# Lightning attention and a leaky-ReLU feed-forward in one Trainium2 kernel: some places of a hand-written order are exchanged

## The chip, the cores and the metric

The kernel runs on one NeuronCore of one Trainium2 chip. The metric is device time in microseconds: the median over runs of the same kernel, smaller is better. The core has a matrix engine (TensorE, PE in the profile, with its weight loads as PEld), a vector engine (VectorE, DVE), a scalar engine (ScalarE, ACT), a general one (GpSimd, POOL) and SyncE (SP), which in this kernel issues nearly all of the DMA transfers, one after the other, from one queue. Each engine runs its own instructions in their order and waits on semaphores for the others.

## What is computed

The reference is block-wise attention with a decaying state, then a two-layer feed-forward. Shapes: 4 batches, 8 heads, 768 positions, 64 per head; the feed-forward takes 3072 tokens of 512, a hidden width of 2048, and gives 3072 x 512, all in 32-bit floats.

```python
for b in range(nb):                      # blocks of 64 positions, per batch and head
    intra = (q_b @ k_b.T) * Dmask        # lam ** (i - j) below the diagonal
    out_b = intra @ v_b + (q_b * lam_pow) @ kv_state
    kv_state = lam ** 64 * kv_state + (k_b * rev_pow).T @ v_b
x = out.transpose(0, 2, 1, 3).reshape(3072, 512)
h = x @ w_in                             # 512 x 2048
y = np.maximum(0.01 * h, h) @ w_out      # 2048 x 512
```

The two weight matrices arrive as 64-bit floats.

## The kernel before, in words

**Tiling.** The tokens are handled as 24 chunks of 128 (two attention blocks each; six chunks make a batch, numbered c = 0 to 23), four chunks make a group g of 512 tokens, and the hidden width is cut into eight blocks p of 256. The feed-forward's operands are split in three parts (h, l, m for x as xh, xl, xm, and for the weights as wh, wl, wm), so that each product of 32-bit precision is made of three products on PE.

**Stages.** Per chunk: load k, q and v; transpose k and q on PE (`transposes`, L550) or, for q of chunks 8 and 9 and for most of the later q and k, load them in 32 KB blocks (`load_subs`, L513) in such an arrangement that DVE can finish the transpose (`turn`, L522); the scores and the state's increment (`scores`, L410), their masking and the state's update (L643, L648, L650 on DVE, L653 on POOL); the outputs (`outputs`, L410), where a tiny copy L682 lies between two halves of the matmuls; and the split of the outputs into xh (L698, ACT), xl (L706, DVE) and xm (L724, DVE). k is scaled in place (L591) and q into another buffer (L598). Per weight block p: two 512 KB loads of 64-bit words (`to_float32`, L787), their conversion with three steps on ACT (L799, L801, L803) and two on DVE (L805, L806), and the split into wh, wm, wl (`parts`, L813 or L815, L818, L820). Per group and block: twelve matmuls per half (`up`, L856), an eviction with the leaky ReLU on ACT (L883), and a store of the result to a DRAM buffer G (L886). After about 340 us the second layer (`down`, L922) reads G back, splits it (L903, L904, L906) and multiplies.

**What sets the order.** No step is issued where it stands in the code. `Plan.add` numbers the operations in the order in which the code creates them, and `emit` issues them in the order of the list `ORDER` (L266): its 1296 entries are pairs of an operation's number and its engine, and a negative number stands for filler matmuls. What the list leaves out follows by a planner that uses the costs written in the calls of `add`. Only the order within one engine reaches the chip as an order; across engines, dependencies become semaphore waits. But `resolve` hands out the interchangeable buffers (four PSUM banks `pt`, `b10`, `b11`, `b2`; `low0` and `low1`; the raw buffers) in the list's order over all engines, so a changed list can exchange their names:

```python
for at, n in enumerate(program):
    ...
    able = [x for x in self.kinds[s.kind] if holds[x] is None or not holds[x].left]
    s.name = ... min(able, key=lambda x: ended[x])
```

The operations that the change and the steps of the prediction name, with the instruction of the profile and the start of each in the profiled execution of the kernel before:

| operation | engine, line | what it is | start, us |
|---|---|---|---|
| 43, 53 | PE L410, L550 | outputs of chunk 1, first half; transpose of q of chunk 2 | 16.87, 16.28 |
| 97, 104, 96, 98 | ACT L801, L803, L799, L803 | conversions of the first two weight halves | 13.39, 14.01, 14.63, 15.19 |
| 188 | PE L550 | transpose of k of chunk 7 | 47.63 |
| 250 | PE L856 | up, group 0, block 2, product xm, wm, first half | 51.38 |
| 272, 270 | SP L513 | q blocks of chunks 8 and 9 | 44.29, 46.80 |
| 349, 325, 355 | SP L787 | loads of weight halves (block 7, block 4, block 4) | 47.35, 48.77, 57.85 |
| 277 | SP L513 | q block | 47.77 |
| 281, 271, 280, 278 | SP L513 | q blocks | 49.22 to 52.32 |
| 283, 208 | SP L466, L528 | k of chunk 8 (two issues), v of chunk 7 | 52.43, 53.42 |
| 267, 274, 276, 279, 282 | SP L513 | q blocks | 54.53 to 57.76 |
| 268, 273, 269, 275 | SP L513 | q blocks | 58.29 to 60.24 |
| 247 | SP L886 | store of the hidden tokens of group 0, block 0 | 60.28 |
| 304, 303 | SP L466, L528 | k of chunk 9, v of chunk 8 | 60.84, 62.33 |
| 326, 327, 328 | ACT L799, L801, L803 | conversion of load 325 | 54.54, 55.13, 55.78 |
| 255, 351, 288 | ACT L883, L801, L682 | eviction of block 2, second half; conversion of load 349; copy in the outputs of chunk 6 | 56.40, 57.29, 60.20 |
| 202, 197 | DVE L598, L706 | scaling of q of chunk 7; xl of chunk 5 | 58.51, 53.55 |
| 206, 330, 336 | DVE L650, L806, L806 | state of chunk 6; second DVE step of loads 325 and 331 | 55.60, 56.56, 57.19 |
| 337, 338, 339 | DVE L815, L818, L820 | wh, wm, wl of block 4 | 57.90, 59.11, 60.67 |
| 289 | PE L410 | state's increment of chunk 7, which reads v of load 208 | 60.04 |
| 340, 344, 341, 345, 346 | PE L856 | up, group 0, block 4: two products with wh, two with wl, one with wm | 61.18 to 66.02 |
| 305 | PE L550 | transpose of k of chunk 9 (load 304) | 66.89 |

The weight blocks named here are those of `w_in`. Loads 325 and 331 are the two halves of block 4, 349 and 355 those of block 7.

Of the kernel before, what the change touches and what calls it, by code (L numbers as in the profile page):

```python
# [239 lines left out]
def kernel(  # L240
# [117 lines left out]
    plan = Plan(kinds, also, {"k@2": early[0], "v@2": early[0], "k@3": early[1], "v@3": early[1], "q@3": early[2]})  # L358
    plan.fill, plan.idle, plan.warm, plan.order = busy, None if ORDER else busy, 1.3 + 0.22 * WARM, ORDER
    add = plan.add  # L360
# [688 lines left out]
```

## Time and profile before

| | |
|---|---|
| median of 3 runs | 606.58 us (606.28 to 606.84) |
| the profiled execution's own time | 607.09 us |
| its span, first to last instruction | 605.3 us |
| mean granted TensorE clock | 0.999 |
| PE busy | 596.8 us (99% of the span) |
| DVE, ACT, POOL busy | 298.7, 208.9, 73.0 us |
| DMA | 105.18 MB, of it 104.30 MB on SP's queue |

A row of the timeline gives the start and the length in us, the engine (a q behind it: its queue, issuing), the line, the operation, the tiles as out<-in, the shapes and a count; in brackets stands how long the engine was idle before it, and what ended that. Tile names have their buffer numbers left out, so `b` is any of three PSUM banks. Rows of one engine that follow each other closely with the same line and tiles are merged. The row of a DMA on SP covers only its issue; the time to landing stands in the rows on DMA issues.

### The profile page before, as it was taken

The numbers are of one execution on the slowest core, as the hardware profiler recorded it, in microseconds if no ns is written. First come the engines' busy times: TensorE is split into PE (matmuls) and PEld (weight loads), VectorE is DVE, ScalarE is ACT, GpSimd is POOL, SyncE is SP. The second block draws the span as 40 slices with busy tenths as digits, with TensorE's granted clock in tenths as the row PEclk, the third lists the DMA queues.
The fourth block names the chain that finished last, engine by engine and source line by source line (L and its number), as shares of the span: only waits on it lengthen the run. The fifth ranks groups of instructions, "written<-read, shape, count | busy, mean of one in ns | idle before, by whom it ended". The sixth has DMA issues, their size and how long they took to land.

```text
span 605.3 us, 12711 instructions
## 1 busy us (share of the span) xinstructions
PE 596.8 (99%) x5362; PEld 491.9 (81%) x5362; DVE 298.7 (49%) x410; ACT 208.9 (35%) x322; POOL 73.0 (12%) x85
## 2 busy tenths in 40 slices
PE   8899999999999999999999999999999999999997
PEld 5787788888888888887888888888888888888886
DVE  6999755360454434344166855354353543534430
ACT  3676661212433433435334421222312313214111
POOL 3332132241322032140000000000000000000000
PEclk9999999999999999999999999999999999999999
DMA  9998887597888798664875833424433333434201
GB/s 219 225 271 190 232 248 198 89 256 180 222 223 203 225 251 236 176 208 175 322 267 181 307 105 125 154 90 138 120 113 131 115 129 122 124 103 125 84 1 69
DMA packets 149993, 105.18 MB, mean 174 GB/s; under 512 B 125872, under 2 KB 126640, under 8 KB 149936
## 3 DMA queue, kind: packets, MB, share of 16 engines
q1 hardware_dynamic: 149648, 104.30, 59.8%
q8 instruction: 42, 0.69, 0.5%
q14 instruction: 15, 0.12, 0.1%
q10 hardware_dynamic: 288, 0.07, 0.0%
HBM read 68.69 MB, written 35.65 MB: 172 GB/s over the span
## 4 chain that ended last, share of the span: by engine, by line
PE 93%; DMA 3%; SPq 2%; DVE 1%; issue 1%; POOL 0%; DVEq 0%; POOLq 0%
PE b L856 31%; PE b L922 16%; PE psc L922 11%; PE po L922 11%; PE pt L856 10%; PE pt L922 5%; PE po L410 4%; PE psc L410 3%; DMA att<-in_k_dram 3%; SPq L513 1%; PE b L349 1%; PE po L550 1%; PE b L550 0%; POOL att L591 0%; PE pt L349 0%
## 5 line engine op out<-in xcount | busy, mean ns | idle before, releaser
L904 DVE SCALAR_TENSOR_TENSOR xl<-att,xh 128x1024 fp32r<-128x1024 f32 x48 | 58.6, 1222 | 125.8 <-ACT xh L903 125.8
L903 ACT ACTIVATE xh<-att 128x1024 fp32r<-128x1024 f32 x48 | 50.9, 1061 | 147.5 <-PE po L922 73.9
L856 PE MATMUL b<-xl,wl 128*128 128x512 f32 (+1 forms) x296 | 78.1, 389 | 0.0
L856 PE MATMUL b<-xm,wm 128*128 128x512 f32 (+1 forms) x296 | 77.8, 390 | 0.0
L856 PE MATMUL b<-xh,wh 128*128 128x512 f32 (+1 forms) x296 | 77.3, 389 | 0.0
L883 ACT ACTIVATE gs<-b 128x512 f32<-128x512 f32 x73 | 42.9, 596 | 95.7 <-PE b L856 85.4
L856 PEld LDWEIGHTS b<-xl,wl 128*128 128x128 f32 x296 | 54.7, 188 | 11.6 <-DVE wl L820 0.4
L856 PEld LDWEIGHTS b<-xh,wh 128*128 128x128 f32 x296 | 54.5, 188 | 11.5 <-DVE att L598 0.3
L856 PEld LDWEIGHTS b<-xm,wm 128*128 128x128 f32 x296 | 54.4, 188 | 11.3
L906 DVE SCALAR_TENSOR_TENSOR xm<-xl,xh 128x1024 fp32r<-128x1024 f32 x48 | 58.8, 1225 | 4.7
L922 PE MATMUL b<-wh,xh 128*128 128x512 f32 x144 | 56.0, 389 | 0.0
L922 PE MATMUL b<-wl,xl 128*128 128x512 f32 x144 | 56.0, 389 | 0.0
L922 PE MATMUL b<-wm,xm 128*128 128x512 f32 x144 | 56.0, 389 | 0.0
L653 POOL TENSOR_TENSOR att<-att 128x256 f32<-128x256 f32 x40 | 29.1, 728 | 112.5 <-DVE att L650 76.6
L922 PE MATMUL psc<-wm,xm 128*128 128x512 f32 (+1 forms) x100 | 38.2, 387 | 0.0
L922 PE MATMUL po<-wm,xm 128*128 128x512 f32 (+1 forms) x100 | 37.9, 384 | 0.0
L922 PE MATMUL psc<-wh,xh 128*128 128x512 f32 x96 | 37.3, 389 | 0.0
L922 PE MATMUL psc<-wl,xl 128*128 128x512 f32 x96 | 37.3, 389 | 0.0
L922 PE MATMUL po<-wh,xh 128*128 128x512 f32 x96 | 37.3, 389 | 0.0
L922 PE MATMUL po<-wl,xl 128*128 128x512 f32 x96 | 37.3, 389 | 0.0
L410 PEld LDWEIGHTS po<-att 64*64 64x64 f32 x1408 | 26.9, 134 | 10.4 <-issue 8.0
L410 PE MATMUL po<-att 64*64 64x64 f32 x1408 | 32.9, 222 | 1.6 <-issue 0.9
(103 smaller groups left out, 858.9 us busy)
## 6 DMA issues: line engine op xcount, KB each, us to landing
att<-g SPq DMA_DIRECT2D x48, 512.0 KB, 3.4
g<-gs SPq DMA_DIRECT2D x47, 512.0 KB, 3.6
raw<-in_moe_w_in_dram SPq DMA_DIRECT2D x16, 512.0 KB, 5.4
raw<-in_moe_w_out_dram SPq DMA_DIRECT2D x16, 512.0 KB, 4.5
out_dram<-gs SPq DMA_DIRECT2D x23, 256.0 KB, 2.1
att<-in_k_dram SPq DMA_DIRECT2D x44, 128.0 KB, 4.0
att<-in_v_dram SPq DMA_DIRECT2D x22, 256.0 KB, 4.3
wo<-w SPq DMA_DIRECT2D x8, 512.0 KB, 3.9
```

Source lines behind the costliest of these rows:

```text
L349: nc.tensor.matmul(wide[:, :k, :], lhsT=ident, rhs=_bc(ident[:, 0:C2], 1, k), start=True, stop=True, skip_group_check=True)
L410: nc.tensor.matmul(dst[HALF[cols]], lhsT=lhsT[HALF[rows]], rhs=rhs[HALF[rows]], start=start, stop=True, skip_group_check=True)
L513: move(0.55, lambda o=o, z=z: nc.sync.dma_start(out=o.rearrange("j (m i) -> j m i", i=C4), in_=z.rearrange("(m j) i -> j m i", j=C4)), key ...
L550: nc.tensor.transpose(out=at[y], in_=src[:, 2 * y:2 * y + 2, :].rearrange("p a d -> p (a d)"), identity=ident)
L653: add("POOL", 0.62, lambda new=new, j=j: nc.gpsimd.tensor_tensor(state[(j + 1) % 4], new, _bc(lam_c, 2, D), op=ALU.mult), [f"st{j % 4}", " ...
L856: nc.tensor.matmul(dst, lhsT=w[z][:, kk * 2 * P + f * P:kk * 2 * P + (f + 1) * P], rhs=x[z][:, kk, toks], start=start and kk == 0, stop=kk ...
L883: add("ACT", ns, lambda b=b, r=r: nc.scalar.activation(out=r(), in_=b(), func=AF.Prelu, bias=0.0, scale=1.0, alpha=0.01), [kb], [kg], rank ...
L903: add("ACT", 1.05, lambda: nc.scalar.activation(out=h, in_=graw[j], func=AF.Copy, bias=0.0, scale=NEAR), reads, wr("h"))
L904: add("DVE", 1.215, lambda: nc.vector.scalar_tensor_tensor(l, graw[j], 1.0, h.bitcast(F32), op0=ALU.mult, op1=ALU.subtract), reads + [f"rh ...
L906: add("DVE", 1.215, lambda: nc.vector.scalar_tensor_tensor(m, l.bitcast(F32), -S, h.bitcast(F32), op0=ALU.mult, op1=ALU.add), [f"rh{j}", f ...
L922: nc.tensor.matmul(to[:, cols], lhsT=ring[j][z][:, f * T + tb * P:f * T + (tb + 1) * P], rhs=W[pp][z][:, f * d_model:(f + 1) * d_model][:, ...
```

## The change

Nothing but the list `ORDER` differs: 34 stretches of it, from entry 49 on to entry 318. No operation is added or removed, and no other line changes. What that does to each engine's own order:

- PE: 43 comes ahead of 53; 250 comes ahead of 188 and the outputs and scores behind it.
- ACT: 97 comes behind 104 and 96; 288 comes ahead of 351.
- DVE: 202 comes ahead of 197; 336 comes ahead of 206 and 330.
- SP, from load 154 (v of chunk 6) to load 303: before 272, 270, 349, 277, 325, 281, 271, 280, 278, 283, 208, 267, 274, 276, 279, 282, 355, 268, 273, 269, 275, 247, 304; after 275, 349, 277, 272, 270, 271, 278, 276, 280, 283, 325, 281, 267, 208, 268, 274, 279, 282, 355, 273, 247, 269, 304.
- POOL: the same.
- Buffers: for block 4, 340 now writes bank `pt` and 344 bank `b10` (exchanged), and `low0` and `low1` are exchanged from 351 on; the later users of both follow.

The other moved entries (51, 119, 71) pass only entries of other engines. The list around the changes, its lines broken here and equal stretches left out:

```diff
...
 (37, "DVE"), (102, "ACT"),
+(51, "DMA"),
 (39, "POOL"), (25, "DVE"), (105, "DVE"), (-6, "PE"), (42, "PE"),
-(53, "PE"),
 (43, "PE"), (103, "ACT"),
-(51, "DMA"), (97, "ACT"),
 (104, "ACT"), (96, "ACT"), (171, "DMA"),
+(97, "ACT"),
 (40, "DVE"), (106, "DVE"),
+(53, "PE"),
 (52, "PE"), (98, "ACT"),
...
 (114, "PE"), (79, "POOL"),
+(119, "DMA"),
 (63, "DVE"), (64, "POOL"),
...
 (81, "PE"), (88, "PE"),
-(119, "DMA"),
 (84, "DVE"), (175, "DVE"),
...
 (116, "ACT"), (215, "DMA"),
-(71, "DVE"),
 (217, "ACT"), (123, "PE"),
+(71, "DVE"),
 (166, "PE"), (94, "DVE"),
...
 (231, "ACT"), (154, "DMA"),
+(275, "DMA"),
 (248, "PE"), (226, "ACT"),
...
 (249, "PE"), (153, "DVE"),
+(250, "PE"),
 (152, "DVE"), (234, "DVE"),
...
 (190, "PE"), (191, "PE"),
-(272, "DMA"), (270, "DMA"),
 (349, "DMA"), (277, "DMA"),
...
 (195, "PE"), (235, "DVE"),
+(272, "DMA"), (270, "DMA"), (271, "DMA"), (278, "DMA"), (276, "DMA"), (280, "DMA"), (283, "DMA"),
 (325, "DMA"), (236, "DVE"),
...
 (201, "DVE"), (333, "ACT"),
-(250, "PE"),
 (199, "ACT"),
-(271, "DMA"),
 (261, "PE"), (204, "DVE"), (251, "ACT"),
-(280, "DMA"),
 (237, "DVE"), (205, "POOL"),
-(278, "DMA"),
 (334, "ACT"),
-(283, "DMA"),
 (238, "DVE"),
+(267, "DMA"),
 (208, "DMA"), (332, "ACT"),
+(202, "DVE"),
 (254, "PE"),
+(268, "DMA"),
 (197, "DVE"), (326, "ACT"),
-(267, "DMA"),
 (203, "DVE"), (335, "DVE"), (257, "PE"), (274, "DMA"),
+(279, "DMA"),
 (329, "DVE"), (327, "ACT"), (262, "PE"), (258, "PE"),
+(336, "DVE"),
 (263, "PE"),
-(276, "DMA"),
 (284, "PE"), (259, "PE"),
...
 (206, "DVE"), (330, "DVE"),
-(336, "DVE"),
 (287, "PE"), (289, "PE"), (290, "PE"), (255, "ACT"),
-(351, "ACT"), (279, "DMA"),
 (337, "DVE"), (282, "DMA"), (288, "ACT"),
-(202, "DVE"),
+(338, "DVE"), (351, "ACT"), (339, "DVE"),
 (355, "DMA"),
-(338, "DVE"), (268, "DMA"), (339, "DVE"),
 (273, "DMA"),
+(247, "DMA"),
 (269, "DMA"),
+(304, "DMA"),
 (207, "POOL"), (291, "PE"), (298, "DVE"), (340, "PE"), (344, "PE"),
-(275, "DMA"),
 (299, "DVE"), (292, "ACT"), (296, "POOL"),
-(247, "DMA"),
 (356, "ACT"), (341, "PE"), (439, "DVE"),
-(304, "DMA"),
 (350, "ACT"), (295, "ACT"),
...
```

2 lines of the change are left out of this document (1 added, 1 removed).

## Prediction

> **What bounds the kernel now.** I read the page's busy shares first, then the busy time by stretch, then TensorE's (PE) timeline for its idle gaps, and only then the SyncE queue (SP) and the vector engines around those gaps. A step named by a number is the operation of that number in the plan, as the table before this prediction lists them.
>
> ```profile
> span 605.3 us, 12711 instructions
> PE 596.8 (99%) x5362; PEld 491.9 (81%) x5362; DVE 298.7 (49%) x410; ACT 208.9 (35%) x322; POOL 73.0 (12%) x85
> ...
> 60.00:70.00 10.00, 9.13 (x232) 7.49 (x226) 6.33 (x11) 5.43 (x11) 2.31 (x3) 1.00 0.90 250
> 130.00:340.00 210.00, 210.00 (x2220) 173.55 (x2219) 93.88 (x155) 80.89 (x139) 36.51 (x41) 1.00 0.77 225
> ```
>
> In the last two rows (stretch, length, then busy time of PE, PEld, DVE, ACT, POOL, the clock, the DMA share) PE is busy all of 130 to 340 us: nothing there can absorb a shift, and the order of PE's work in it is unchanged. So a microsecond won or lost by PE before 70 us should reach the end whole. The change reorders work only between about 14 and 67 us, so PE's gaps in that stretch are all that can be won:
>
> ```profile
> 46.25 1.07 PE L856 MATMUL b<-xl,wl 128*128 128x512 f32 x4
> 47.63 0.75 PE L550 MATMUL po<-att 128*128 128x128 f32 x4 [0.32 <-DMA att<-in_k_dram]
> ...
> 51.38 1.09 PE L856 MATMUL b<-xm,wm 128*128 128x512 f32 x4
> 52.31 1.08 PE L856 MATMUL b<-xh,wh 128*128 128x512 f32 x4
> ...
> 59.98 0.98 PE L410 MATMUL psc<-att 64*64 64x64 f32 x54
> ...
> 61.18 1.19 PE L856 MATMUL b<-xh,wh 128*128 128x512 f32 x4
> ...
> 63.13 1.08 PE L856 MATMUL b<-xl,wl 128*128 128x512 f32 x4
> ...
> 64.95 1.07 PE L856 MATMUL pt<-xm,wm 128*128 128x512 f32 x4
> 66.89 0.76 PE L550 MATMUL po<-att 128*128 128x128 f32 x4 [0.87 <-DMA att<-in_k_dram]
> ```
>
> Both gaps (in brackets) stand before a transpose of k (188 at 47.63, 305 at 66.89) whose load comes late. 1.19 us together is nearly all there is.
>
> **Part 1: PE 43 ahead of 53, and the conversion step 97 two places later on ScalarE (ACT).** 97, 104 and 96 only change places among themselves on ACT; the last of the group, 98, still comes after the same work, so that costs 0. On PE the transpose 53 now comes behind the 16 small matmuls of 43:
>
> ```profile
> 16.87 0.46 PE L410 MATMUL po<-att 64*64 64x64 f32 x16
> 16.98 0.69 DVE L531 COPY att<-b 128x512 f32<-128x512 f32 x1 [0.65 <-PE b L550]
> 18.00 1.06 POOL L591 TENSOR_TENSOR gs<-gs,att 128x512 f32<-128x512 f32 x1 [1.19 <-PE pt L550]
> 18.14 1.47 DVE L806 CUSTOM_DVE_ANT_0 w<-w,low 128x1024 uint16<-128x1024 uint16 x1
> 20.73 0.74 PE L856 MATMUL pt<-xh,wh 128*128 128x256 f32 x4 [0.63 <-ACT wh L813]
> ```
>
> 53's reader, the copy at 16.98, had already waited for it, and behind that copy VectorE (DVE) has the L806 that leads to wh, for which PE waits at 20.73. So up to 0.46 us, the length of the 16 matmuls, goes onto the path. But that L806 takes 1.47 us with a POOL instruction running from 18.00 to 19.06 beside it, where two of them take 1.30 together further down (56.56). If it only gets going when POOL ends, starting it at 18.6 ends it at about 19.7 instead of 19.61. I take +0.1; ends 0 and +0.46. The Trainium skill ("SBUF — State Buffer", section "SBUF: two separate sides") calls that pair an exclusive lock held for the whole instruction; the 1.47 us row agrees, and without the lock the sum would take the +0.46.
>
> **Part 2: the product 250 ahead of the transpose 188.** 250 takes 0.93 us (51.38 to 52.31), its operands are older than those of the product at 46.25 (its wm is made ahead of that wl), and PE is idle for 0.32 us there: −0.32, ends −0.32 and 0. Work behind 188 comes 0.61 us later up to the old place of 250 (51.38); its readers on ACT and DVE hand nothing back that PE wants within the next two products, and those 1.9 us are the cover. If they are gone, the 0.61 comes back as a wait. The DVE swap of 202 ahead of 197 goes with this: 197 waits for that later work.
>
> **Part 3: the SP queue.** Now SP's order decides.
>
> ```profile
> 44.29 2.94 SPq L513 DMA_DIRECT2D att<-in_q_dram  x2
> 47.35 0.39 SPq L787 DMA_DIRECT2D raw<-in_moe_w_in_dram  x1
> 47.77 0.47 SPq L513 DMA_DIRECT2D att<-in_q_dram  x1
> 48.77 0.39 SPq L787 DMA_DIRECT2D raw<-in_moe_w_in_dram  x1
> 49.22 3.10 SPq L513 DMA_DIRECT2D att<-in_q_dram  x4
> 52.43 0.93 SPq L466 DMA_DIRECT2D att<-in_k_dram  x2
> 53.42 0.73 SPq L528 DMA_DIRECT2D att<-in_v_dram  x1
> ...
> raw<-in_moe_w_in_dram SPq DMA_DIRECT2D x1, 512.0 KB, 4.0
> raw<-in_moe_w_in_dram SPq DMA_DIRECT2D x1, 512.0 KB, 5.7
> raw<-in_moe_w_in_dram SPq DMA_DIRECT2D x1, 512.0 KB, 4.5
> att<-in_v_dram SPq DMA_DIRECT2D x1, 256.0 KB, 4.1
> ```
>
> The last four rows are single issues with the time to landing: the weight loads issued at 47.35 (349), 48.77 (325) and 57.85 (355), and the v load at 53.42 (208). Load 325 falls behind five more 32 KB blocks of q and the two issues of k load 283. A block costs 0.47 (row 47.77) to 0.78 (3.10 for 4), the k issues 1.0: 325 is issued at 48.77 + 3.4 = 52.2 up to 53.9; I take 52.8. It lands 4.0 to 5.7 us later; I take 4.5, the row whose queue is nearest to the new place, with small blocks ahead: 57.3 against 54.5, ends 56.2 and 59.6. Load 208 follows two q blocks behind it, at about 54.3, and lands at 58.4; PE takes that v at 60.0 (step 289, in the row 59.98), so 1.6 us cover it, and if they are gone, 289 waits for the rest.
>
> Who waits for 325:
>
> ```profile
> 54.54 0.69 ACT L799 ACTIVATE w<-raw 128x512 f32<-128x512 f32 x1 [0.25 <-DMA raw<-in_moe_w_in_dram]
> 55.78 0.75 ACT L803 ACTIVATE low<-raw 128x512 f16<-128x512 f32 x1
> 56.40 0.56 ACT L883 ACTIVATE gs<-b 128x512 f32<-128x512 f32 x1
> ...
> 56.56 1.30 DVE L806 CUSTOM_DVE_ANT_0 w<-w,low 128x1024 uint16<-128x1024 uint16 x2 [0.55 <-ACT low L803]
> 58.51 0.68 DVE L598 TENSOR_TENSOR att<-pt,att 128x512 f32<-128x512 f32 x1
> 59.11 1.53 DVE L818 SCALAR_TENSOR_TENSOR wm<-wh,w 128x1024 fp32r<-128x1024 f32 x1
> 60.67 1.22 DVE L820 SCALAR_TENSOR_TENSOR wl<-wm,wh 128x1024 fp32r<-128x1024 f32 x1
> ```
>
> ACT stands on 326 (54.54) until 57.3; 328 (55.78) then ends at 59.3 instead of 56.53. Queued behind on ACT: the eviction 255 (56.40), now near 59.2; its bank was next written by 340 (61.18), and the exchanged bank names give it to 344, one product later, near 62, so 0. The copy 288 behind it, which PE needs at once, is now ahead of 351 and just fits at 60.2. On DVE 328 feeds an L806 (330). Before, 5.36 us passed from 328's end to the end of wl of block 4 (339, 61.89). The change puts half of the 1.30 (336) and the 0.60 of the row 58.51 (202) ahead of the wait: 5.36 − 0.65 − 0.60 = 4.1, so wl ends at 59.3 + 4.1 = 63.4. PE wanted it at 63.13 and would now, by parts 1 and 2, want it at 62.9: a new wait of some 0.6 us (with 0.1 of passing on) for 341. From there to transpose 305 is 2.9 us of PE (63.13 to the end of 64.95's row): PE reaches 305 at 66.4.
>
> **Part 4: k load 304 behind the same transfers, with store 247 and block 269 exchanged ahead of it.**
>
> ```profile
> 60.84 1.26 SPq L466 DMA_DIRECT2D att<-in_k_dram  x2
> ...
> 60.84 5.92 DMA att<-in_k_dram
> ...
> att<-in_k_dram SPq DMA_DIRECT2D x44, 128.0 KB, 4.0
> ```
>
> The second row is from the chain of waits, 5.92 us from issue to landing, after which PE's 0.87 of idle time ends; the third is the page's, the median of all such loads. The set of transfers ahead of 304 on the queue is the same, so its turn comes at the same time unless the queue was idler or busier on the way; its issue also needs PE's 289, at about 60.6. The landing lies between 60.6 + 4.0 = 64.6 and the old 66.8. Since less waits in the queue when the q blocks go out alone early, I take 66.0. Then wl, not k, ends last: 305 starts at 66.4 instead of 66.89. The store 247 ahead of 269 frees a gs buffer for an eviction off the path (0); the last q block now lands after that store, and its reader, a DVE transpose at 65, has over 2 us before PE asks for it (0, or the excess over that).
>
> **The sum.** +0.1 − 0.32 by 60 us, then a wait of 0.6 in place of one of 0.87: 66.4 − 66.89 = −0.5 us. The profiled span of 605.3 becomes 604.8, and its execution of 607.09 becomes 606.6. That execution lies 0.5 us over the median of the three runs, 606.58; from the median, 606.1. Exchanged names of PSUM banks and of the two low buffers cost 0: same engines and shapes. A measurement of this kernel can tell about 0.2% (1.2 us) from no change.
>
> **Rivals.** Slower, by the late weights: each microsecond that 325 lands after 57.3 delays wl and PE one for one. From 57.8 on the kernel is slower than before; at the late end, 59.6, it is 606.1 + 2.3 = 608.4. For it speaks that ACT already waits 0.25 us for this load and that the load's own row, 5.7, is the longest; against it the spare 1.2 us between wl's end and PE's use. Faster than can be doubted: 325 lands by 56.2, so wl is no wait, and k lands by 65.5; then both gaps go, 0.1 − 0.32 − 0.87 = −1.1, to −1.3 where part 1 costs nothing and the ends of the matmuls are counted by starts: 605.3. It needs every row at its good end. Nothing but the first gap: k lands 66.8 as before, 305 keeps its clock time, and the kernel gains 0 to 0.1: 606.5, inside the forecast's own range.
>
> **How the numbers follow.** Forecast and the third rival, both within 0.2%: 0.50; their range 605.5 to 607.5. Slower by more than 1.2 us needs 325 landing past 59.0, or a later v or k besides, in a queue that the change has made less even: 0.31. Faster by more than 1.2: 0.19, as no more than 1.3 can be won. The range 605.2 to 608.4 takes in both ends; beyond the upper one a second wait, on v for 289, would have to come on top.
>
> **What will show it.** Right: no idle PE before the transpose that was at 47.63; ACT's first L799 on the moved load waiting 2 to 3 us; an idle PE of 0.3 to 0.9 before the L856 on wl that was at 63.13, and less than 0.87 before the next transpose. Wrong: that L799 waiting under 1 us (325 was not held up), PE waiting for v at 60, or k still 5.9 us on the way.

## The result and the profile after

The changed kernel takes 609.5 us (median of 7 runs, 609.08 to 610.13) against 606.84 us of the kernel before beside it (7 runs, 605.88 to 608.78): a ratio of 1.0033 with a 95% interval of 1.0018 to 1.0047, so some 2 us slower (1.1 to 2.9; the two medians lie 2.7 apart). Forecast was 606.1 us with 605.2 to 608.4 as the range. The profiled execution took 610.13 us, the longest of the seven; its span is 608.4 against 605.3.

The page of the changed kernel and its busy time by stretch (start:end, length, then PE, PEld, DVE, ACT, POOL, the clock, the DMA share, GB/s):

```profile
span 608.4 us, 12712 instructions
PE 596.0 (98%) x5362; PEld 491.7 (81%) x5362; DVE 300.7 (49%) x410; ACT 208.2 (34%) x322; POOL 74.2 (12%) x85
...
52.00:54.00 2.00, 2.00 (x11) 1.62 (x9) 1.97 (x2) 2.00 (x5) 1.44 (x1) 1.00 0.29 43
58.00:60.00 2.00, 2.00 (x38) 1.46 (x39) 0.00 (x0) 0.44 (x1) 0.00 (x0) 1.00 0.86 186
60.00:62.00 2.00, 0.79 (x46) 0.66 (x40) 1.73 (x4) 2.00 (x6) 0.29 (x1) 1.00 0.73 121
...
60.00:70.00 10.00, 7.38 (x126) 5.70 (x116) 9.49 (x14) 7.39 (x14) 3.74 (x4) 1.00 0.88 234
130.00:340.00 210.00, 210.00 (x2290) 173.67 (x2282) 93.35 (x154) 80.90 (x140) 38.75 (x43) 1.00 0.76 225
```

From 130 to 340 us PE is busy all the time, as before. The loss is in the stretch from 60 to 70 us: PE is idle for 2.62 of 10 us, where it was idle for 0.87. PE's own rows (start, length, line, in brackets the idle time ahead and what ended it):

```profile
16.62 0.69 PE L410 MATMUL po<-att 64*64 64x64 f32 x32 [1.71 <-issue]
...
49.04 0.60 PE L550 MATMUL po<-att 128*128 128x128 f32 x4
...
61.68 1.16 PE L410 MATMUL psc<-att 64*64 64x64 f32 x64 [1.21 <-DVE att L650]
...
63.33 1.20 PE L856 MATMUL pt<-xh,wh 128*128 128x512 f32 x4 [0.26 <-DVE wh L815]
...
66.59 1.20 PE L856 MATMUL pt<-xl,wl 128*128 128x512 f32 x4 [1.15 <-DVE wl L820]
...
69.45 0.60 PE L550 MATMUL po<-att 128*128 128x128 f32 x4
...
129.72 1.16 PE L410 MATMUL psc<-att 64*64 64x64 f32 x64 [0.82 <-POOL att L591]
```

Both waits for k of the kernel before (0.32 ahead of the transpose now at 49.04, 0.87 ahead of the one now at 69.45) are gone. In their place stand three new ones: 1.21 us ahead of 289 (61.68), 0.26 ahead of 340 (63.33), 1.15 ahead of 341 (66.59), together 2.62 us. The same steps stood at 59.98, 61.18, 63.13 and 66.89 (the transpose 305) before: the shift is 1.70, 2.15, 3.46 and, since k is no longer waited for, 2.56 us. Two gaps that lie outside the changed work are longer too: the standstill that ends at 16.62 (1.71, before 0.91) and the one that ends at 129.72 (0.82, before 0.21). Whether these belong to the change, only further runs can tell.

How the three came about, from the changed kernel's timeline of SP, ACT, DVE and POOL in turn, with the issue rows of load 325 and of the v load 208 (last column: us to landing):

```profile
43.95 3.95 SPq L513 DMA_DIRECT2D att<-in_q_dram  x1
48.02 0.37 SPq L787 DMA_DIRECT2D raw<-in_moe_w_in_dram  x1
48.44 4.53 SPq L513 DMA_DIRECT2D att<-in_q_dram  x7
53.09 0.93 SPq L466 DMA_DIRECT2D att<-in_k_dram  x2
54.11 0.46 SPq L787 DMA_DIRECT2D raw<-in_moe_w_in_dram  x1
54.62 0.95 SPq L513 DMA_DIRECT2D att<-in_q_dram  x2
55.62 1.84 SPq L528 DMA_DIRECT2D att<-in_v_dram  x1
...
59.56 0.67 ACT L799 ACTIVATE w<-raw 128x512 f32<-128x512 f32 x1 [4.44 <-DMA raw<-in_moe_w_in_dram]
...
60.27 0.43 DVE L805 TENSOR_SCALAR w<-w 128x512 int32<-128x512 int32 x1 [3.52 <-ACT w L799]
60.61 0.68 DVE L806 CUSTOM_DVE_ANT_0 w<-w,low 128x1024 uint16<-128x1024 uint16 x1
61.21 0.41 DVE L650 TENSOR_TENSOR att<-att,psc 128x256 f32<-128x256 f32 x1
61.55 0.69 DVE L806 CUSTOM_DVE_ANT_0 w<-w,low 128x1024 uint16<-128x1024 uint16 x1
62.28 1.00 DVE L815 CAST wh<-w 128x1024 fp32r<-128x1024 f32 x1
63.31 1.97 DVE L818 SCALAR_TENSOR_TENSOR wm<-wh,w 128x1024 fp32r<-128x1024 f32 x1
65.31 1.23 DVE L820 SCALAR_TENSOR_TENSOR wl<-wm,wh 128x1024 fp32r<-128x1024 f32 x1
...
61.70 1.02 POOL L653 TENSOR_TENSOR att<-att 128x256 f32<-128x256 f32 x1 [8.17 <-DVE att L650]
62.69 1.51 POOL L591 TENSOR_TENSOR att<-att 128x512 f32<-128x512 f32 x1
...
raw<-in_moe_w_in_dram SPq DMA_DIRECT2D x1, 512.0 KB, 5.4
...
att<-in_v_dram SPq DMA_DIRECT2D x1, 256.0 KB, 5.0
```

Load 325 is issued at 54.11 instead of 48.77, behind seven q blocks (4.53 us for 224 KB) and the k load; ahead of them and of 349, block 275 alone held SP for 3.95 us (43.95). It lands 5.43 us later, at 59.54. Once load 349 had landed (52.28), only those small blocks and then k were left to move, and the DMA engines ran dry: their share from 52 to 54 us is 0.29 at 43 GB/s, where the kernel before had this row:

```profile
52.00:54.00 2.00, 2.00 (x11) 1.62 (x10) 1.97 (x3) 1.67 (x4) 0.55 (x1) 1.00 0.91 231
```

ACT then stands for 4.44 us in front of 326. DVE stands for 3.52 us in front of 329, which needs 326 (its busy time from 58 to 60 is 0.00). Behind 329 on DVE stand not only the steps of the weights but also 206, the L650 at 61.21: it reads the PSUM tile `psc`, which PE's 289 is about to write. In the kernel before it ran at 55.60. The change also put 336, the L806 at 60.61, ahead of it, which makes 0.60 of its lateness. The chain of waits of the changed kernel goes the same way:

```profile
54.11 5.43 DMA raw<-in_moe_w_in_dram
...
60.27 0.43 DVE w L805
...
65.31 1.24 DVE wl L820
...
66.59 1.20 PE pt L856 x4
```

### The profile page after: what moved, and what is told of

Read it like the earlier page. It is cut to its first block, busy times and chain, and to the rows that moved or that the text cites. A ratio compares the mean times of both kernels' runs of the same rounds, so it can differ in the third digit from the quotient of the medians.

```text
span 608.4 us, 12712 instructions
## 1 busy us (share of the span) xinstructions
PE 596.0 (98%) x5362; PEld 491.7 (81%) x5362; DVE 300.7 (49%) x410; ACT 208.2 (34%) x322; POOL 74.2 (12%) x85
## 4 chain that ended last, share of the span: by engine, by line
PE 90%; SPq 3%; DVE 3%; DMA 2%; issue 1%; POOL 0%; ACT 0%; DVEq 0%; POOLq 0%
PE b L856 30%; PE b L922 16%; PE psc L922 11%; PE po L922 11%; PE pt L856 10%; PE pt L922 5%; PE po L410 4%; PE psc L410 3%; SPq L513 3%; DMA raw<-in_moe_w_in_dram 1%; DMA att<-in_k_dram 1%; DVE wm L818 0%; DMA att<-in_lam_dram 0%; PE b L550 0%; PE po L550 0%
## 5 line engine op out<-in xcount | busy, mean ns | idle before, releaser
L856 PE MATMUL b<-xl,wl 128*128 128x512 f32 (+1 forms) x300 | 79.4, 390 | 0.0
L856 PE MATMUL b<-xh,wh 128*128 128x512 f32 (+1 forms) x300 | 78.9, 389 | 0.0
L653 POOL TENSOR_TENSOR att<-att 128x256 f32<-128x256 f32 x40 | 29.6, 741 | 116.3 <-DVE att L650 78.1
```

Of the source, the lines that this page charges most:

```text
L653: add("POOL", 0.62, lambda new=new, j=j: nc.gpsimd.tensor_tensor(state[(j + 1) % 4], new, _bc(lam_c, 2, D), op=ALU.mult), [f"st{j % 4}", " ...
L856: nc.tensor.matmul(dst, lhsT=w[z][:, kk * 2 * P + f * P:kk * 2 * P + (f + 1) * P], rhs=x[z][:, kk, toks], start=start and kk == 0, stop=kk ...
```

## The experiments

The theory: the late load 325 makes the loss, through the vector steps behind 329. Its rivals: the order of 53 and 43 makes a part of it; the v load 208 and not 206 holds 289; the gaps at 16 and 129 us belong to the new order. Ratios below are to the kernel before run beside each, with 95% intervals.

**The two ends of part 1.** The changed kernel with 53 back, and the kernel before with 53 moved:

```diff
 (42, "PE"),
+(53, "PE"),
 (43, "PE"),
...
 (106, "DVE"),
-(53, "PE"),
 (52, "PE"),
```

> The changed kernel with the transpose 53 put back ahead of the outputs 43 on PE; nothing else. In the changed kernel PE reaches the first product of block 1 (operation 155, waits for wh through L805, L806, L813) 0.98 us later than in the kernel before. Theory A (the order of 53 and 43 costs only its matmuls): 0.2 to 0.5 us come back there, about 0.5 us of PE's idle time ahead of the outputs at 16.6 us stays, and the time falls from 609.5 to about 609.1. Theory B (PE's standstill of 1.71 us ahead of these outputs belongs to the new order): 0.9 to 1.0 us come back, 608.5. Theory C (the standstill is a chance of the run, as PE's own code arrives): its length, 0.91 before and 1.71 after, is a third value here, and the start of that product goes with it.

> The kernel before with only PE's 53 moved behind 43. Theory A (the 16 matmuls ahead of 53 pass through): the first product of block 1 starts 0.2 to 0.5 us later than the 20.73 of the kernel before, and the time is about 607.2 against 606.8. Theory of the prediction (the L806 with POOL beside it absorbs it): at most 0.1 us later, 606.9. Theory B (the new order brings a longer standstill of PE): 1.0 us later, 607.8.

Measured: 609.82 us, ratio 1.0034 (1.0018 to 1.0050), with 53 put back; 607.27 us, ratio 0.9998 (0.9986 to 1.0009), with 53 alone moved. Neither move of 53 changes the time by more than the noise, which is some 0.7 to 1.0 us to each side here. PE's rows of the first kernel and then of the second:

```profile
15.74 0.46 PE L410 MATMUL po<-att 64*64 64x64 f32 x16 [0.87 <-issue]
20.59 0.73 PE L856 MATMUL pt<-xh,wh 128*128 128x256 f32 x4 [0.25 <-ACT wh L813]
...
61.67 1.16 PE L410 MATMUL psc<-att 64*64 64x64 f32 x64 [1.39 <-DVE att L650]
```

```profile
15.54 0.69 PE L410 MATMUL po<-att 64*64 64x64 f32 x32 [0.58 <-issue]
...
20.64 0.74 PE L856 MATMUL pt<-xh,wh 128*128 128x256 f32 x4 [0.43 <-ACT wh L813]
```

The standstill at 16 us is 0.87 with the old order of 53 and 0.58 with the new one, so the 1.71 of the changed kernel was a chance of that run: theory C. Over all 14 profiles of this document it is 0.58 to 1.71 with the new order of 53 and 0.77 to 1.32 with the old. It also did not matter: with 1.1 us won by 20.59, this kernel waits at 61.67 until the same moment as the changed one, because the late load, which lands at 59.52 here, sets it. The gap near 129 us differs from run to run as well: over the 14 profiles it lies between nothing and 0.86 us in the changed kernel and its variants, and between nothing and 0.56 in the kernel before and its own. Whether the new order adds some tenths of a microsecond there, these profiles don't tell. What the order itself costs is small: from the end of the outputs 42 to the start of 53 it is −0.07 and −0.06 us with the old order (the kernel before, and the one with 53 put back) and +0.16 in both with the new one.

**The late load undone, in the changed kernel.**

```diff
 (272, "DMA"), (270, "DMA"),
+(325, "DMA"),
 (271, "DMA"), (278, "DMA"), (276, "DMA"), (280, "DMA"), (283, "DMA"),
-(325, "DMA"),
 (236, "DVE"),
```

> The changed kernel with the weight load 325 issued ahead of q block 271 again, so with five q blocks ahead of it as before instead of ten transfers more; nothing else. Theory (the late load is the cause of PE's waits at 60 to 67 us): it lands by about 55.5 instead of 59.5, DVE's 206 starts by 57, wh and wl of block 4 come in time, and PE's idle times ahead of 289, 340 and 341 (1.21 + 0.26 + 1.15 = 2.62 us) all go; the wait for k of chunk 9 comes back with 0.5 to 1.0. Time 609.5 - 2.62 + 0.8 = 607.7, between 607.0 and 608.2. Rival (the v of chunk 7, load 208, landed at 60.58 in the changed kernel, holds 289): an idle time of 0.8 or more stays ahead of 289, and the time is 608.5 or more.

Measured: 607.13 us, ratio 0.9992 (0.9977 to 1.0008): the whole loss is gone. The load lands at 55.79 and 206 starts at 58.13, later than the 57 expected. From 59 to 70 us PE has one wait left:

```profile
67.64 0.73 PE L550 MATMUL po<-att 128*128 128x128 f32 x4 [0.87 <-DMA att<-in_k_dram]
```

The wait for k of chunk 9 is back at 0.87, about as the theory had it. The v load landed at 60.49 here, nearly as late as in the changed kernel (60.58), and 289 follows its predecessor without a wait of 0.2 or more, as PE gets there only at 60.62.

**The late load alone, in the kernel before.**

```diff
 (235, "DVE"),
-(325, "DMA"),
 (236, "DVE"),
...
 (283, "DMA"),
+(325, "DMA"),
 (238, "DVE"),
```

> The kernel before with only the weight load 325 moved behind the load 283, so behind five transfers. Theory (the late load alone makes the loss): issued near 52, it lands at 57 to 58; DVE's 329 and the 206 behind it start 3 us late, near 58.5; PE's 289 waits not at all or a little (0 to 0.5), 340 and 341 wait 0.3 and 0.5 to 1.1 us together; the wait for k of chunk 9 (0.87) falls by as much as it can. Net slower by 0.3 to 1.5 us: 607.2 to 608.3 against 606.8. Rival (only the whole new order of the queue makes the load so late): landing before 56.5 and a time within 0.2 us of the kernel before.

Measured: 608.46 us, ratio 1.0032 (1.0022 to 1.0043). This one move gives as much as the whole change, a little more than expected. Load 325 lands at 57.03 in its profile, and PE waits for the weights but not ahead of 289:

```profile
62.01 1.21 PE L856 MATMUL b<-xh,wh 128*128 128x512 f32 x4 [0.50 <-DVE wh L815]
65.00 1.21 PE L856 MATMUL b<-xl,wl 128*128 128x512 f32 x4 [0.86 <-DVE wl L820]
```

The new waits are 1.36 us, and the 0.87 for k is gone: 0.5 net, and its span is 605.9 against 605.3. That is less than the 1.8 us between the medians. The profiled run was 607.72, which is 0.7 under this kernel's median, and the profile of the kernel before lies 0.5 above the median of its first three runs; with both the accounts come near each other, but how late the load is in a typical run, the one trace doesn't show.

**Why 289 waits: 206 or v.** First 206 alone ahead of 329 on DVE, then the v load alone ahead of two q blocks, then both, each in the changed kernel:

```diff
 (279, "DMA"),
+(206, "DVE"),
 (329, "DVE"),
...
 (328, "ACT"),
-(206, "DVE"),
 (330, "DVE"),
```

```diff
 (236, "DVE"),
+(208, "DMA"),
 (281, "DMA"),
...
 (267, "DMA"),
-(208, "DMA"),
 (332, "ACT"),
```

> The changed kernel with the state's update 206 (DVE) put ahead of 329, which waits for the late load; nothing else. Theory (289 waits because 206 stands behind 329 on DVE): PE's idle time ahead of 289 falls from 1.21 to at most 0.3, 206 runs near 56 to 57, but what is won is lost again ahead of 340 and 341, whose weights come at most 0.4 us earlier: 609.1, between 608.7 and 609.6. Rival (289 waits for the v load 208): the 1.21 stays and nothing moves, 609.5. Second rival (the waits add up): 289's wait goes and those of 340 and 341 stay as they are, 608.4.

> The changed kernel with only the v load 208 ahead of the q blocks 281 and 267 on SP's queue, still behind the late load 325; DVE's 206 stays behind 329. Theory (289 had two late inputs, and 206 ends last): v lands before 60 us, PE's idle time ahead of 289 stays at 1.2 to 1.5 with the state's update L650 as what ended it, and the time stays at 1.003 of before, 608.4 to 609.4. Rival (v alone held 289): the idle time falls to 0.5 or less and the time by 0.5 to 1.0.

> The changed kernel with 206 ahead of 329 on DVE (as in the run of that alone) and besides the v load 208 ahead of the q blocks 281 and 267 on SP's queue, still behind the late load 325. Theory (289 had two late inputs, 206 and the v, and with 206 early the v load held it alone): v lands 0.5 to 1.2 us earlier and PE's idle time ahead of 289 falls from 1.50 to 0.3 to 1.0; what is won goes mostly into the waits for wh and wl of block 4, and the time is 607.8 to 608.2 against 608.1 of that run. Rival (the v load is held by something else than its place): the landing stays at 60.5 to 61.6 and nothing changes.

With 206 early: 608.11 us, ratio 1.0009 (0.9995 to 1.0022). With v early: 609.13 us, 1.0025 (1.0016 to 1.0034). With both: 607.37 us, 1.0018 (1.0004 to 1.0032), which the first can't be told from. The rows of PE, DVE and POOL with 206 early, then PE's with v early, then those of ACT and PE with both:

```profile
61.70 1.16 PE L410 MATMUL psc<-att 64*64 64x64 f32 x64 [1.50 <-DMA att<-in_v_dram]
65.35 1.20 PE L856 MATMUL pt<-xl,wl 128*128 128x512 f32 x4 [0.22 <-DVE wl L820]
...
56.35 0.41 DVE L650 TENSOR_TENSOR att<-att,psc 128x256 f32<-128x256 f32 x1
...
62.08 0.69 DVE L815 CAST wh<-w 128x1024 fp32r<-128x1024 f32 x1
62.81 1.23 DVE L818 SCALAR_TENSOR_TENSOR wm<-wh,w 128x1024 fp32r<-128x1024 f32 x1
...
56.84 0.62 POOL L653 TENSOR_TENSOR att<-att 128x256 f32<-128x256 f32 x1 [3.62 <-DVE att L650]
```

```profile
60.80 1.16 PE L410 MATMUL psc<-att 64*64 64x64 f32 x64 [0.57 <-DVE att L650]
```

```profile
57.38 0.67 ACT L799 ACTIVATE w<-raw 128x512 f32<-128x512 f32 x1 [2.64 <-DMA raw<-in_moe_w_in_dram]
...
63.87 1.19 PE L856 MATMUL pt<-xl,wl 128*128 128x512 f32 x4 [0.41 <-DVE wl L820]
```

289 had two late inputs: in the changed kernel v landed at 60.58 and 206 ended at 61.62. With 206 out of the way it waits for v, which landed at 61.56 in that run; with v early (59.41) it waits for 206, for 0.57 us instead of the 1.2 to 1.5 expected, as load 325 landed at 58.66 there. With both early it doesn't wait; but load 325 landed at 57.35 in that profile, 2.2 us earlier than in the changed kernel, so how much of this the two moves do, the profile doesn't show. So my expectation that 206 alone would free 289 was wrong, and so was the rival that v alone would. Still the first run is faster than the changed kernel (1.0009 against 1.0033, just clear of the noise), by another way, as its profile has it: 206 early lets POOL's L653 behind it run early, at 56.84 for 0.62 us, and DVE's wh and wm then have no POOL instruction beside them: 0.69 and 1.23 us instead of 1.00 and 1.97. wl is ready at 65.29 instead of 66.54, and 341's wait falls from 1.15 to 0.22.

**The product 250 ahead of 188, alone; and then the product 342 ahead of 305 as well.**

```diff
 (153, "DVE"),
+(250, "PE"),
 (152, "DVE"),
...
 (333, "ACT"),
-(250, "PE"),
 (199, "ACT"),
...
 (346, "PE"),
+(342, "PE"),
 (305, "PE"),
...
 (400, "DMA"),
-(342, "PE"),
 (360, "DVE"),
```

> The kernel before with only the product 250 moved ahead of the transpose 188. Theory of the prediction: the idle 0.32 us ahead of 188 goes, everything behind it is 0.3 us earlier, and the time falls by about 0.3. Rival, from the runs so far (k of chunk 9 has landed at its own time, 66.5 to 69.2 us, whatever PE did): PE is 0.3 us earlier until 60 us, the wait ahead of the transpose 305 grows from 0.87 to about 1.2, and the time stays what it was, within 0.1 us.

> The kernel before with the product 250 ahead of the transpose 188 and, in the same way, the last product 342 of block 4 ahead of the transpose 305: both of PE's waits for a late k get a product of 0.9 us whose operands are there. Theory (the loads of k land at their own times and products fill the waits): both idle times, 0.32 and 0.87 us, go, and the kernel is 1.0 to 1.2 us faster than before: 605.7 against 606.8. Rival (the wait moves on to the next load or vector step): idle time of like size appears behind 305 before 130 us, and the time stays within 0.3 us.

Measured: 606.40 us, ratio 1.0001 (0.9990 to 1.0012), for 250 alone; 606.53 us, 1.0001 (0.9991 to 1.0011), with both. Neither shows a gain. For both together the interval rules out the 1.0 to 1.2 us expected; the 0.3 us expected of 250 alone is too small for it. With both, the two waits for k are gone from the profile, and a new one stands two steps on:

```profile
69.58 1.66 PE L856 MATMUL b<-xh,wh 128*128 128x512 f32 x6 [0.72 <-ACT xh L698]
```

342 had covered the split of the outputs into xh (L698) before the product 395. Used ahead of 305, it is missing there. The rival had it so.

**The kernel before once more.**

> The kernel before once more, unchanged, for a second profile of it. Theory (PE's standstill ahead of the outputs of chunk 1 follows the arrival of a piece of its own code, and is a chance of the run): that gap lies anywhere from 0.6 to 1.7 us and ends 1.2 to 1.45 us after the end of the first transfer on the instruction queue; the waits for k ahead of 188 and 305 come out at 0 to 0.6 and 0.6 to 1.2. Rival (these are fixed by the order): 0.9, 0.3 and 0.9 again, within 0.1. The time is the same as before, within 0.1%.

Measured: 606.97 us, ratio 0.9997 (0.9987 to 1.0008). Its waits, in the unchanged order:

```profile
48.65 0.72 PE L550 MATMUL po<-att 128*128 128x128 f32 x4 [0.92 <-DMA att<-in_k_dram]
67.18 0.75 PE L550 MATMUL po<-att 128*128 128x128 f32 x4 [0.20 <-DVE att L522]
```

0.32 and 0.87 have become 0.92 and 0.20, and with 53 alone moved they were nothing and 0.79: how large each of the two waits is, is in good part a chance of the run.

**An earlier k.** The store 247 behind the k load 304 and the v load 303, with the eviction 260 behind the copy 309; and the same in the changed kernel, with 325 and 206 put right as above.

```diff
 (296, "POOL"),
-(247, "DMA"),
 (356, "ACT"),
...
 (303, "DMA"),
+(247, "DMA"),
 (357, "ACT"),
...
 (456, "DVE"),
-(260, "ACT"),
 (310, "PE"),
...
 (309, "ACT"),
+(260, "ACT"),
 (359, "DVE"),
```

> The kernel before with the store 247 behind the k load 304 and the v load 303 on SP's queue, and on ACT the eviction 260, which needs that store, behind the small copy 309; nothing else. Theory (the k of chunk 9 shares the DMA engines with what was issued ahead of it): k lands 0.5 to 1.0 us earlier, the wait ahead of 305 falls from 0.87 to 0 to 0.4, and the time by 0.4 to 0.8. Rival (the bytes on the way and not the order set the landing): k lands as before and nothing is won. Rival 2 (the eviction 260, late now, holds the split of the outputs 313 and so the product 395): what is won at 305 is lost ahead of 395.

> The changed kernel with three places put right: the weight load 325 ahead of 271 again, 206 ahead of 329 on DVE, and the store 247 behind 304 and 303 with the eviction 260 behind 309. Theory (the losses of the changed kernel are the late load and the vector steps behind it; its gain is the product 250 ahead of 188): none of PE's waits ahead of 289, 340, 341 is left, the one ahead of 305 is under 0.5, and the time is 606.0 to 606.6, 0 to 0.6 under before. Rival (what the late load cost comes back as a later k of chunk 9, as in the run with the load alone put back): 0.9 ahead of 305, and the time of that run, 0.9992 of before.

Measured: 606.43 us against 607.44, ratio 0.9989 (0.9978 to 1.0000), and 607.03 us, 0.9993 (0.9979 to 1.0007). In the first, k lands 4.97 us after its issue at 61.06 (6.33 before), and the transpose follows at once:

```profile
65.53 1.07 PE L856 MATMUL pt<-xm,wm 128*128 128x512 f32 x4
66.44 0.60 PE L550 MATMUL po<-att 128*128 128x128 f32 x4
```

That is the best version found. Its gain of 0.1% is at the edge of what was measured. The other has no PE wait of 0.3 us or more left from 30 to 126 us either, but one of 0.86 at 126.79, ended by POOL's L591, and is no faster than the kernel before as far as the interval tells.

## Why the prediction was wrong

**What bounds the kernel** was read rightly: after 130 us nothing absorbs a shift, and the work that moved PE lies ahead of 70 us. The step that starts at 126.69 before starts at 129.72 after, 3.03 us later, and the profiled span is 3.1 longer; in none of the 14 profiles is PE idle for 0.15 us or more at once after 134 us.

**Part 1** (+0.1, ends 0 and +0.46). The size was inside the bounds: 53 starts 0.23 us later against the outputs ahead of it, and the first product of block 1 comes 4.45 to 4.48 us after 53 in both orders, so it passes on whole. The reason given failed: "If it only gets going when POOL ends" assumed that POOL's instruction stays where it was, but it waits for PE too and moved with it (18.00 to 18.42), and now falls on the L805 ahead of that L806: L805 takes 1.21 us instead of 0.42, and L806 runs alone behind it, in 0.69 instead of 1.47. That the number lay inside the bounds is luck. In the time of the kernel, part 1 is too small to be told (0.9986 to 1.0009 for it alone).

**Part 2** (−0.32). The wait went, as said, but no gain is shown: 250 alone measures 1.0001, and 0.3 us (0.0005) lies inside its interval. The wait at 188 came out at 0.92 and 0.76 in two other runs of the old order there and under 0.2 in two more, and the later steps depend on loads that come when they come. A gap of one trace was taken for a price.

**Part 3** is the step that failed. It named the right mechanism, the late weights, and its rival had the right sign, but the price of the late load came out too small.

The term outside its bounds is the chain behind the load: "5.36 − 0.65 − 0.60 = 4.1" from 328's end to wl's end was 5.02 (61.52 to 66.54). Of the 0.9 between, 0.31 + 0.44 are wh and wm, slowed by POOL's instructions beside them (1.00 instead of 0.69, 1.97 instead of 1.53). POOL's L653 and L591 stood there because of a waiter that the text put at nothing: it lists 255, 288 and 330 behind the late load, but not 206, which stood behind 329 and 336 on DVE, and for which L653 waited 8.17 us. The other runs bear this out: the chain took 5.01 and 5.02 us where 206 was late too (53 put back, v early), and 3.97 and 4.47 where it was early (206 alone, both).

The two terms ahead of the chain came out late. The issue of 325: forecast at 52.8, at most 53.9 (five times 0.78 and 1.0 give 53.7), came at 54.11. Block 275, now first, held SP for 3.95 us, so that 349 went out at 48.02 instead of 47.35, and with 272 and 270 moved behind 349 six blocks more than before stood between it and 325 (the prediction counted five, 275 among them). The landing: "I take 4.5", and it took 5.43, so 59.54, at the late end given. This is partly a chance of the run: with the same order of the queue up to 325, five profiles (the changed kernel, 53 put back, 206 early, v early, both) have the issue at 51.77 to 54.51 and the landing at 57.35 to 59.54. The kernels differ elsewhere, but their profiled times follow the landing: 606.37 us at 57.35, 608.73 at 58.66, 608.98 at 59.34, 609.70 at 59.52, 610.13 at 59.54. In the earliest, near the forecast 57.3, 340 and 341 waited 0.16 and 0.41, about the 0.6 of the forecast, with 206 and v early.

The v load, forecast at 58.4, landed at 60.58, so its cover of 1.6 us was gone as well. The wait of 289 itself added nothing, as wl came later still: with 206 early it was longer (1.50), and the kernel faster. By the prediction's own rule, a landing of 59.54 gave 606.1 + 2.24 = 608.3; the chain's 0.9 puts it at 609.2, and the measured 609.5 is that within the spread.

**Part 4.** The two halves of k of chunk 9 landed at 67.84 and 68.22 and not at 66.0, as their issue, which needs 289, came at 62.20. PE was later still (69.45), so that wait did go, as forecast, but not because k came earlier; its 0.87 paid a part of the 2.62.

**The signs.** The idle time at the transpose 188 went, as listed. L799 waited 4.44 us and not 2 to 3, and the product with wl 1.15 and not 0.3 to 0.9. Of the signs of being wrong, PE did wait at 60 us, but 206 ended that wait and not v.

## What to carry to other kernels

When a load is moved back, list everything that stands behind its first consumer on each engine, not only what the load feeds: a short step that frees another engine's buffer is as late as the load. Small transfers put ahead of a large one cost their issue time, not their bytes: here most blocks of 32 KB held SP for 0.31 to 0.47 us, as long as a load of 512 KB. An idle gap ahead of an engine in one trace is a gain only if the next late input isn't already waiting behind it; a second profile of the same kernel shows how much of the gap is fixed. A gain of 0.3 us can be argued from a trace of this kernel, but the time doesn't confirm it: the intervals here reach some 0.5 to 1.0 us to each side.

## What the runs showed of the hardware

**PE's first standstill ends shortly after a piece of code has arrived.** In all 14 profiles PE stands idle ahead of the second half of the outputs 42, for 0.58 to 1.71 us, with nothing shown that ends it. In each, the first transfer of 16 KB on the queue that the profile calls "instruction" ended shortly before: at 14.56 in the kernel before, 15.24 in the changed one, 14.21 in the run with 53 alone moved; PE goes on at 15.89, 16.62 and 15.54, and over all 14 it goes on 1.20 to 1.51 us after that end. No run changed that transfer by itself, so the cause is argued and not shown. The Trainium skill ("Runtime: NRT & Kernel Launch", section "Instruction fetch mechanics") calls the crossing of such a 16 KiB block mostly hidden; if this is one, the gaps here disagree.

**Vector and general engine slow each other.** wm takes 1.97 us and wh 1.00 with POOL's L591 and L653 beside them, 1.23 and 0.69 without; these POOL instructions take 1.51 and 1.02 us beside DVE, 1.06 and 0.62 without. The Trainium skill ("SBUF — State Buffer", section "SBUF: two separate sides") calls the shared port an exclusive lock for the whole instruction: by that wm, begun when L591 ends at 64.20, would end at 65.43; it ended at 65.28, so the trace agrees within 0.15 us.

**Small transfers can leave the DMA engines short of work.** Seven q blocks of 32 KB hold SP for 4.53 us, ten times as long as the issue of one load of 512 KB (0.46 us), and the DMA share falls to 0.29 from 52 to 54 us; it fell to 0.30 at the same place with 53 put back, and to 0.29, from 50 to 52, with 206 and v early. The issue of a block is not always short: six of the seven take 0.31 to 0.47 us, the last 1.29, and the block 275 ahead of them 3.95. What makes an issue long, no run shows.
